# Attention and gated MLP on one core: the second head's softmax scaling in blocks 3 to 5 moved from ScalarE to GpSimd

## The chip, the cores and the metric

The kernel runs on one core of one Trainium2 chip. The metric is device time in microseconds (us) of one execution. The engines are named as in the profile: PE is TensorE's matmul stream and PEld its weight loads, DVE is VectorE, ACT is ScalarE, POOL is GpSimd, SP is SyncE, which here issues the DMAs. SBUF is the on-chip memory; a PSUM bank is where PE writes its results.

## The reference

Attention with a local window and a few global columns, over 4 batches, 8 heads, 768 positions and 64 channels, then a two-layer MLP whose gate is h times sigmoid(h), on 3072 tokens.

```python
scores = scale * np.matmul(q, k.transpose(0, 1, 3, 2))
...
keep = is_global | is_local            # 8 global columns, 96 local positions
...
scores = np.where(keep, scores + bias, -1000000000.0)
a = np.exp(scores - np.max(scores, axis=-1, keepdims=True))
a = a / (np.sum(a, axis=-1, keepdims=True) + 1e-09)
x = np.matmul(a, v)                    # then (B, H, S, D) -> (3072, 512)
...
h = x @ w_in                           # 512 -> 2048
g = h * (1.0 / (1.0 + np.exp(-h)))
return (g @ w_out).astype(np.float32)  # 2048 -> 512
```

The line that the change touches is the division of `a` by its row sums.

## The kernel before

**Tiles.** The queries are cut into 24 blocks of 128 positions (`i`, six to a batch), and the 8 heads of a block into 4 pairs (`hp`), so there are 96 pair steps, numbered `u = 4 * i + hp`. Blocks 3 to 5 are the steps 12 to 23. A block sees 232 columns (96 before it, 8 global, its own 128), so a head's probabilities are a tile of 128 x 232 in float32; the two heads of a pair lie side by side in one tile `pe`.

**A pair step.** PE makes the scores in a bank (L626 in the blocks up to 5). DVE adds the bias and takes the row's extreme (L639, one instruction for each head). ACT takes the exponential and its row sum (L647). DVE adds 1e-9 to the two sums (`guard`, L654) and inverts them (`inverse`, L658). Then `norm` multiplies each head's tile by its inverse sum, one value for each of the 128 rows: head 0 on DVE (L669), head 1 on DVE too, but in blocks 3 to 5 on ACT (L667), which `on_act` and the parameter `NA=(12, 24)` say. PE turns both heads (`turn_p`, L683, up to four transposes into one bank), ACT moves the result to SBUF (`move_p`, L693), and PE multiplies by the values (L708).

**The MLP.** Two blocks make a group of 256 tokens (`g`, 12 groups). The weights come as raw 64-bit words in 32 pieces and are built up by DVE: three bit operations (L416, L422, L428), a rounding copy by ACT (L440) and a subtraction by DVE (L444), which leave a high and a low part of each piece in SBUF. Groups 0 and 1 use the weights as they come: for each of 16 slices `f`, PE makes h with 12 matmuls (L869), ACT and DVE gate it (L875, L879) and split it into two parts (L883, L887), and PE multiplies by the second weight (L894, 6 matmuls). The later groups use another form of the second product (L972, L978, L984, L990, L1020, L1049), in which POOL adds 128 x 128 tiles (L990).

**The order.** Nothing is ordered by hand on an engine. `Plan` is a list scheduler that runs while the program is built: each step has an engine, a planned cost in ns, a rank, the steps that it needs and the buffers that it uses. `run` goes through planned time, gives each free engine the ready step of lowest rank, and emits the steps in that order; on the chip each engine then works through its own queue in that order. A planned cost therefore changes the order on all engines from the first place where it matters. The step of `norm` is made in the loop over `i` and `hp`; `guard` and `inverse` are ahead of it, and `turn_p` needs both heads:

```python
o = op("DVE", 72, u - PAR["RI"], (lambda i=i, hp=hp: inverse(i, hp)), [o], [pe])
...
o = op("PE", 438 if j else 220, u - PAR["RP"], (lambda i=i, hp=hp, tp=tp: turn_p(i, hp, tp)), [*o, joint], [pe, tp])
```

The functions that the diff touches, with what calls them:

Of the kernel before, what the change touches and what calls it, by code (L numbers as in the profile page):

```python
# [17 lines left out]
ALU = mybir.AluOpType  # L18
# [11 lines left out]
PAR = dict(  # L30

    LAT=140, SD=125, DL=1900, D0=2700, DW=2900, DO=3400, MG=60, T2=45000, LAT2=230, MG2=400, F0=600, F1=1200, C1=900, C2=2300, COLD=8000, WEND=8600,

    CAP=dict(po=4, av=2, s=4, h=3, tp=2, tq=4), HU=13,

    C0=14, CR=1, LW=1, LB=5, QB=3.5, RI=2.8, RN=2.8, RP=0.2, RM=0, RV=1.2, RQ=0.1, RB=3, LK=-25, LAG=1,

    BP=(4, 3), NX=20, CF=8, AHEAD=5, SB=(4,), LQ=(1, 2), CN=3, I0=6, QS='ACT', G0=2, TR=10, RL=4500, TL=6000, CL=3200, VC=8, WT=2, HE=1.8, TP=3, ORD=(5, 7, 0, 1, 2, 3, 4, 6), NA=(12, 24), V2=6,
)


# [9 lines left out]
class Plan:  # L51
# [31 lines left out]
    def op(self, eng, cost, rank, emit, deps=(), uses=(), lat=None):  # L83
        o = dict(eng=eng, cost=int(cost), rank=rank, emit=emit, uses=list(uses), lat=lat,
                 need=0, ready=0, then=[], n=len(self.ops))
        o["uses"] += [b.also for b in o["uses"] if b.also]
        for d in deps:
            if d is not None:
                d["then"].append(o)
                o["need"] += 1  # L90
        for b in o["uses"]:
            b.n = min(b.n, len(self.ops))
            b.left += 1
        self.ops.append(o)
        return o
# [90 lines left out]
def attn_moe(ctx, tc, q, k, v, n_global, n_local, w_in, w_out, out):  # L186
    nc = tc.nc
# [3 lines left out]
    NHP = H // 2  # L191
# [165 lines left out]
    op = plan.op  # L357
    FIRST = -1e6
    DVE = lambda n: 1000 * (62 + n) / 960
    ACT = lambda n, over=61: 1000 * (over + n) / 1200  # L360
# [86 lines left out]
    for n in range(2 * NFC):  # L447
        rank = PAR["C0"] + PAR["CR"] * n
        a, m, x = [] if lent(n) is not None else [Buf("big")], Buf("mid", "m"), lent(n)
        o = op("DMA", 1456, rank - PAR["LW"], (lambda n=n: stage(n, "w")), [o_l[x]] if not a else (), a, PAR["DW"])  # L450
        o_st.append(o)
        o = op("DVE", 335, rank, (lambda n=n: conv1(n)), [o], [*a, m])
        o = op("DVE", 602, rank, (lambda n=n: conv2(n)), [o], [*a, m])
        o = op("DVE", 602, rank, (lambda n=n: conv3(n)), [o], [*a, m])
# [32 lines left out]
    for n in range(2 * NFC):  # L487
        a = Buf("ck", "big")
        o = op("DMA", 1456, 1e6 + n, (lambda n=n: stage(n, "c")), [o_c[-4]] if n > 1 else (), [a], PAR["CL"])
# [3 lines left out]
    for n in range(PAR["VC"] // 2):  # L493
        a = Buf("ck", "big")
        o = op("DMA", 1456, 1e6 + 99 + n, (lambda n=n: check_v(n)), [o_c[-1]], [a], PAR["CL"])
# [160 lines left out]
    def inverse(i, hp):  # L656
        t = blk[i]
        nc.vector.reciprocal(t["inv", hp], t["inv", hp])  # L658

    def on_act(u):  # L660
        return (1,) if PAR["NA"][0] <= u < PAR["NA"][1] else ()

    def norm(i, hp, a):
        t = blk[i]
        x = t["p", hp][:, a, :cols(i)[1]]
        if a in on_act(NHP * i + hp):
            nc.scalar.mul(x, x, t["inv", hp][:, a:a + 1])  # L667
        else:
            nc.vector.tensor_scalar(x, x, t["inv", hp][:, a:a + 1], None, ALU.mult)  # L669
# [71 lines left out]
    for i in range(B * NJ):  # L741
        j, g = i % NJ, i // NB
        rank = NHP * i - PAR["QB"]
        ob, kk, lr = o_k[i], kb[i], PAR["LB"]
        if not i:
            xn, later = dict(k=Buf("qkn", "m"), q=Buf("qkn", "m")), []
            for p0, p1 in PARTS:
                for nm in "kq":
                    n, tp = p1 - p0, Buf("tq")
                    hi = kk[nm.upper() + "H"]  # L750
                    o = op("DMA", 364 * n, -8.5, (lambda nm=nm, a=2 * p0, b=2 * p1: load(0, nm, a, b)), (), [xn[nm]], PAR["D0"])
                    rank = 0.2 if p0 else rank
                    o = op("PE", 110 * n, rank, (lambda nm=nm, tp=tp, a=p0, b=p1: turn(0, nm, tp, a, b)), [o], [xn[nm], tp, hi])
# [3 lines left out]
        for nm in "kq" if i else "":  # L757
            xn, tp = Buf("big") if in_kind(i, nm) == "big" else Buf("qkn", "m"), Buf("tq")
            hi, lo = kk[nm.upper() + "H"], kk[nm.upper() + "L"]
            o = op("DMA", 1456, rank - lr if i < NJ + NB else FIRST + rank, (lambda i=i, nm=nm: load(i, nm)), () if i < NJ + NB else [before["t"]], [xn], PAR["DL"])  # L760
# [5 lines left out]
            o = op("PE", 440, rank, (lambda i=i, nm=nm, tp=tp: turn(i, nm, tp)), [o, *own, *o_w[-PAR["WT"]][i != PAR["I0"]:]] if stacked else [o], [xn, tp, hi, lo] if stacked else [xn, tp, hi])  # L766
# [35 lines left out]
        for hp in range(NHP):  # L802
            u = NHP * i + hp
            stacked = i >= PAR["I0"]
            kind = pt_kind(i, hp)
            pe, pt, tp = Buf("pe", "m"), Buf(kind, "m" if kind == "pt" else None), Buf("tp")
            n = cols(i)[1]
            hps = (hp,) if stacked or (not i and hp < 2) else (hp - hp % 2, hp - hp % 2 + 1)
            if hp == hps[0]:
                s = [Buf("s") for _ in range(1 if stacked else 2)]  # L810
                ks = [kk[x] for x in (("KH", "KL", "QH", "QL", "R") if stacked else ("KH", "QH"))]
                before["s"] = o_s[u] = op(
                    "PE", 440 if stacked else 390 + len(hps) * (385 if j else 218), u,
                    (lambda i=i, hps=hps, s=s: stack_scores(i, hps[0], s) if i >= PAR["I0"] else scores(i, hps, s)),
                    [x for y, x in ob.items() if i or y[1] <= hps[-1] < y[2]] + [before.get("s")], s + ks,
                )
            o = before["s"]
            if not u:
                for x in later:
                    plan.after(x, o)  # L820
            if u == PAR["HU"] - 1:
                o["hold"] = 1
            o_e = []
            for a in range(2):
                x = op("DVE", 318 if j else 210, u, (lambda i=i, hp=hp, a=a: top_of(i, hp, a)),
                       [o, o_b[j == 0, hp], before.get("top") if not a else None], [s[a % len(s)], pe])
                if not a:
                    before["top"] = x
                o_e.append(op("ACT", ACT(n, 112) + 186, u, (lambda i=i, hp=hp, a=a: expo(i, hp, a)), [x], [pe]))
            if i >= PAR["VC"] and hp == 1:  # L830
                o_c.append(op("DVE", 598, u + 0.5, (lambda i=i: check_here(i)), [arrived, before["top"]], [kk["vn"]]))
            o = op("DVE", 67, u - PAR["RI"], (lambda i=i, hp=hp: guard(i, hp)), o_e, [pe])
            o = op("DVE", 72, u - PAR["RI"], (lambda i=i, hp=hp: inverse(i, hp)), [o], [pe])
            o = [op(*(("ACT", ACT(n)) if a in on_act(u) else ("DVE", 250 if j else 196)), u - PAR["RN"], (lambda i=i, hp=hp, a=a: norm(i, hp, a)), [o], [pe])
                 for a in range(2)]
            o = op("PE", 438 if j else 220, u - PAR["RP"], (lambda i=i, hp=hp, tp=tp: turn_p(i, hp, tp)), [*o, joint], [pe, tp])
            o_m.append(op("ACT", ACT(512 if j else 256), u - PAR["RM"], (lambda i=i, hp=hp, pt=pt: move_p(i, hp, pt)), [o, before.get("move")], [tp, pt]))
            before["move"] = o_m[-1]
            pts.append(pt)
# [11 lines left out]
        if early:  # L851
            x = Buf("pt", "m")
# [68 lines left out]
    G0 = PAR["G0"]  # L921
# [170 lines left out]
    for m0, n in enumerate(PAR["ORD"]):  # L1092
# [3 lines left out]
        o, run = o_first[-1], []  # L1096
        for m, c in enumerate((690, 423, 423)):
# [4 lines left out]
            o = op("DVE", c, rank, emit, [o, o_w[-1][1]], [rb, tb])  # L1102
        o_p.append(o)
        o = op("ACT", 940, rank, (lambda n=n: t_high(n)), [o], [rb, tb])
        hs = op("DMA", 1456, rank, (lambda n=n: t_store(n, 0)), [o], [rb, tb], PAR["TL"])
        o = op("DVE", 1130, rank, (lambda n=n: t_low(n)), [o], [rb, tb])
# [6 lines left out]
    for g in range(NGRP):  # L1113
# [4 lines left out]
        o = o_h[g - 1, NFC - 1] if g > 1 else None  # L1118
        for f in range(NFC) if g < G0 else ():
            rank = 1e3 + (max(g, 1) * NFC + f + (PAR["LAG"] + 0.5 if g else 0))  # L1120
            ph, th, gh, gl = Buf("h"), Buf("th"), Buf("gh"), Buf("gl")
            for c in range(NCC):
                o = op("PE", 349, rank + PAR["LK"] / 10, (lambda g=g, f=f, c=c, h=ph: moe_h(g, f, c, h)),
                       [o, *o_w[2 * f]] + o_x[g], [ph, xb[g]["xh"], xb[g]["xl"]])
# [3 lines left out]
            t = op("ACT", 340, FIRST + rank, (lambda g=g, f=f, b=th: moe_tanh(g, f, b.slot)), [o], [ph, th])  # L1128
            t = op("DVE", 335, FIRST + rank, (lambda g=g, f=f: moe_gate(g, f)), [t], [ph, th])
# [9 lines left out]
        for n in range(NFC // 2) if g >= G0 else ():  # L1139
# [4 lines left out]
            for c in range(2 * NCC):  # L1144
                o = op("PE", 349, rank + PAR["LK"] / 10 - (PAR["HE"] if end else 0), (lambda g=g, n=n, c=c, h=ph: pair_h(g, n, c, h)),
                       [o] + o_x[g], [ph, sg, xb[g]["xh"], xb[g]["xl"]])
# [7 lines left out]
            t = op("ACT", 600, FIRST + rank, (lambda g=g, n=n: pair_tanh(g, n)), [o], [ph, sg])  # L1154
            t = op("DVE", 690, FIRST + rank, (lambda g=g, n=n: pair_gate(g, n)), [t], [ph, sg])
# [6 lines left out]
            for m, (a, b) in enumerate(cuts):  # L1162
                if b == 7:
                    for e in range(4):
                        x = "DVE" if soon and e != 1 else "POOL"
# [76 lines left out]
        if g < G0:  # L1242
            ob = Buf("big")
            for tt in range(NB):
                eng = "ACT" if tt % 2 else "DVE"
                o = op(eng, dict(ACT=478, DVE=598)[eng], FIRST + rank,
                       (lambda g=g, tt=tt: moe_end(g, tt)), [last[tt]], [po[tt], ob])
# [79 lines left out]
    o = steps(judge, [70, 270, 100, 70, 270, 100, 70, 270, 100, 70, 70, 70, 70, 70, 70, 70], -1, o_c + o_x[-1], ())  # L1327
    o = op("PE", 60, -1, verdict, [o], [jb])
# [190 lines left out]
```

## Time and profile before

| | |
|---|---|
| time, median of 3 runs | 672.51 us (671.33 to 672.54) |
| the profiled execution | 671.82 us, of which the span from its first to its last instruction is 670.0 us |
| PE busy | 660.1 us, 99% of the span |
| DVE busy | 545.1 us, 81% |
| ACT busy | 431.8 us, 64% |
| POOL busy | 154.1 us, 23% |
| granted TensorE clock | 1.00 of full speed over the span |

A matmul's record reaches past the start of the next one, since they are pipelined; so the busy share of PE says that it had something in flight, and its real pace is read from the starts. Records of DVE and ACT overlap a little in the same way: what an instruction takes in a queue is the step from its start to the start of the next.

### The profile page before, as it was taken

What the parts mean: (1) busy time and instruction counts of PE and PEld (TensorE: products, weight loads), DVE (VectorE), ACT (ScalarE), POOL (GpSimd) and SP (SyncE); (2) the same over time, 40 slices, a digit from 0 to 9 for tenths busy, and PEclk for the clock granted to TensorE, in tenths of its full rate; (3) what the DMA queues carried; (4) which work ended last, traced back from release to release, by engine and by line L of the source; (5) the groups of instructions that cost most, each with busy time, mean ns of one, the idle gap of its engine ahead of it and who ended that gap; (6) DMA issues with size and microseconds to landing.
All of it is one profiled execution on the core that took longest, in us unless ns stands there. A gap on an engine that the chain in (4) does not pass through costs nothing.

```text
span 670.0 us, 15715 instructions
## 1 busy us (share of the span) xinstructions
PE 660.1 (99%) x5756; PEld 633.7 (95%) x5756; DVE 545.1 (81%) x1507; ACT 431.8 (64%) x1026; POOL 154.1 (23%) x339
## 2 busy tenths in 40 slices
PE   7999999999999999999999999999999999999997
PEld 5778899999999999999999999999999999999997
DVE  6999999998668888878889878877878887975545
ACT  6997544687567676665775766684667666673333
POOL 2100000010003322324322323323332332322331
PEclk9999999999999999999999999999999999999999
DMA  9997757575887589669687686675876788754442
GB/s 184 235 284 256 230 165 241 167 239 181 239 246 250 168 256 283 196 180 295 186 223 235 202 235 198 211 229 170 288 217 185 226 230 217 226 162 144 126 167 82
DMA packets 146068, 141.63 MB, mean 211 GB/s; under 512 B 88356, under 2 KB 115492, under 8 KB 145988
## 3 DMA queue, kind: packets, MB, share of 16 engines
q1 hardware_dynamic: 145984, 140.60, 70.4%
q8 instruction: 46, 0.75, 0.5%
q14 instruction: 34, 0.28, 0.1%
q10 hardware_dynamic: 4, 0.00, 0.0%
HBM read 117.44 MB, written 18.87 MB: 203 GB/s over the span
## 4 chain that ended last, share of the span: by engine, by line
PE 94%; DVE 4%; ACT 1%; DMA 0%; issue 0%; DVEq 0%; ACTq 0%
PE bank L972 33%; PE bank L1049 29%; PE bank L894 7%; PE bank L869 7%; PE bank L708 5%; PE bank L683 5%; PE bank L596 5%; PE bank L528 2%; DVE pe L639 1%; DVE pe L669 1%; DMA qn<-in_q_dram 0%; ACT pe L647 0%; PE bank L1332 0%; DVE wf L428 0%; DVE wf L422 0%; PE bank L626 0%
## 5 line engine op out<-in xcount | busy, mean ns | idle before, releaser
L990 POOL TENSOR_TENSOR sg<-sg 128x128 f32<-128x128 f32 x279 | 128.9, 483 | 285.4 <-DVE sg L984 232.7
L972 PE MATMUL bank<-xh,WIH 128*128 128x256 f32 x640 | 183.1, 286 | 0.0
L972 PE MATMUL bank<-xl,WIH 128*128 128x256 f32 x640 | 177.8, 278 | 0.0
L972 PE MATMUL bank<-xh,WIL 128*128 128x256 f32 x640 | 177.6, 278 | 0.0
L1020 DVE TENSOR_TENSOR gl<-sg,gh 128x512 fp32r<-128x512 f32 (+1 forms) x152 | 97.6, 647 | 34.4 <-ACT gh L1014 30.6
L972 PEld LDWEIGHTS bank<-xl,WIH 128*128 128x128 f32 x640 | 120.6, 188 | 0.5
L972 PEld LDWEIGHTS bank<-xh,WIH 128*128 128x128 f32 x640 | 120.6, 188 | 0.4
L972 PEld LDWEIGHTS bank<-xh,WIL 128*128 128x128 f32 x640 | 120.3, 188 | 0.0
L1014 ACT CAST gh<-sg 128x512 fp32r<-128x512 f32 (+1 forms) x152 | 83.9, 568 | 52.3 <-PE bank L1049 38.6
L647 ACT ACTIVATE pe<-pe,NM 128x232 f32<-128x232 f32 (+1 forms) x192 | 90.2, 473 | 36.6 <-DVE NM L639 35.8
L978 ACT ACTIVATE sg<-bank 128x512 f32<-128x512 f32 x80 | 47.8, 597 | 48.1 <-PE bank L972 47.5
L639 DVE CUSTOM_DVE_ANT_0 pe<-bank,B 128x232 f32<-128x232 f32 (+1 forms) x192 | 66.5, 373 | 12.6 <-PE bank L596 11.8
L1049 PE MATMUL bank<-WOH,gh 128*128 128x256 f32 (+1 forms) x280 | 74.0, 294 | 0.0
L984 DVE SCALAR_TENSOR_TENSOR sg<-sg,bank 128x512 f32<-128x512 f32 x80 | 54.8, 685 | 23.4 <-ACT sg L978 22.7
L1049 PE MATMUL bank<-WOL,gh 128*128 128x256 f32 (+1 forms) x280 | 72.5, 289 | 0.0
L669 DVE TENSOR_SCALAR pe<-pe,sm 128x232 f32<-128x232 f32 (+1 forms) x180 | 60.5, 370 | 1.4
L683 PE MATMUL bank<-ident,pe 128*128 128x128 f32 (+1 forms) x352 | 55.0, 276 | 3.7 <-DVE pe L669 3.5
L693 ACT COPY pt<-bank 128x512 f32<-128x512 f32 (+1 forms) x82 | 44.7, 549 | 15.1 <-PE bank L683 13.0
L1049 PEld LDWEIGHTS bank<-WOH,gh 128*128 128x128 f32 x280 | 52.8, 188 | 1.5 <-issue 0.7
L1049 PEld LDWEIGHTS bank<-WOL,gh 128*128 128x128 f32 x280 | 52.7, 188 | 0.8
L1049 PE MATMUL bank<-WOH,gl 128*128 128x256 f32 (+1 forms) x280 | 49.5, 292 | 0.0
L683 PEld LDWEIGHTS bank<-ident,pe 128*128 128x128 f32 (+1 forms) x352 | 39.9, 136 | 8.9 <-DVE pe L669 6.1
(165 smaller groups left out, 1509.8 us busy)
## 6 DMA issues: line engine op xcount, KB each, us to landing
tx<-ts SPq DMA_DIRECT2D x72, 512.0 KB
ty<-ts SPq DMA_DIRECT2D x72, 256.0 KB
c<-in_moe_w_in_dram SPq DMA_DIRECT2D x16, 512.0 KB
c<-in_moe_w_out_dram SPq DMA_DIRECT2D x16, 512.0 KB
vn<-in_v_dram SPq DMA_DIRECT2D x24, 256.0 KB
w<-in_moe_w_in_dram SPq DMA_DIRECT2D x12, 512.0 KB
w<-in_moe_w_out_dram SPq DMA_DIRECT2D x12, 512.0 KB
kn<-in_k_dram SPq DMA_DIRECT2D x23, 256.0 KB
```

The lines of the kernel that those rows point to most:

```text
L639: nc.vector.tensor_tensor_reduce(t["p", hp][:, a, :n], t["s", hp][a][:, :n], B1[:, hp] if i % NJ else B0[:, hp], -SC / (1 + a), 3.0e38, AL ...
L647: nc.scalar.activation(x, x, AF.Exp, bias=NM[:, i * H + h:i * H + h + 1], scale=-1.0, accum_out=t["sum", hp][:, a:a + 1],)
L669: nc.vector.tensor_scalar(x, x, t["inv", hp][:, a:a + 1], None, ALU.mult)
L683: nc.tensor.transpose(ps[:n, c, a], pe[:, a, c0:c0 + n], ident)
L869: nc.tensor.matmul(ph, w[:, c, fs], x[:, c], start=not c and not n, stop=c == NCC - 1 and n == 2)
L972: nc.tensor.matmul(ph[:, a], w[:, cc, fs], x[:, cc], start=not cc and not m, stop=cc == NCC - 1 and m == 2)
L978: nc.scalar.activation(x[:, 0:4].rearrange("p (a b) c -> p a (b c)", a=2), mo["ph", g, n], AF.Tanh, scale=0.5)
L984: nc.vector.scalar_tensor_tensor(x, x, 1.0, mo["ph", g, n], ALU.add, ALU.mult)
L990: (eng.tensor_sub if e else eng.tensor_add)(x[:, o], x[:, a], x[:, b])
L1014: nc.scalar.copy(mo["gh", g, n][:, a:b], mo["sg", g, n][:, a + o:b + o])
L1020: nc.vector.tensor_sub(mo["gl", g, n][:, a:b], mo["sg", g, n][:, a + o:b + o], mo["gh", g, n][:, a:b].bitcast(F32))
L1049: nc.tensor.matmul(o, l, r, start=(g, b) not in opened, stop=n == NFC // 2 - 1 and m == 2 and (p in ((2, 7, 5, 3, 4) if g == NGRP - 1 else ...
```

## The change

Head 1 of each pair in blocks 3 to 5 is scaled by a GpSimd `tensor_tensor` product instead of a ScalarE `mul`. Its second input is the column of 128 inverse sums, spread along the row by a step of zero. The planned cost of that step becomes 800 ns on POOL, where it was `ACT(n)`, that is 1000 * (61 + 232) / 1200 = 244 ns, on ACT. `NA` stays as it is, but `on_pool` is asked first, and its range is the same.

```diff
-    ... TP=3, ORD=(5, 7, 0, 1, 2, 3, 4, 6), NA=(12, 24), V2=6,
+    ... NP=(12, 24), HE=1.8, TP=3, ORD=(5, 7, 0, 1, 2, 3, 4, 6), NA=(12, 24), V2=6,
...
+    def on_pool(u, a):
+        return a == 1 and PAR["NP"][0] <= u < PAR["NP"][1]
+
...
-        if a in on_act(NHP * i + hp):
+        if on_pool(NHP * i + hp, a):
+            nc.gpsimd.tensor_tensor(x, x, t["inv", hp][:, a:a + 1].to_broadcast(list(x.shape)), ALU.mult)
+        elif a in on_act(NHP * i + hp):
             nc.scalar.mul(x, x, t["inv", hp][:, a:a + 1])
...
-            o = [op(*(("ACT", ACT(n)) if a in on_act(u) else ("DVE", 250 if j else 196)), ...
+            o = [op(*(("POOL", 800 if j else 500) if on_pool(u, a) else ("ACT", ACT(n)) if a in on_act(u) else ("DVE", 250 if j else 196)), ...
```

## Rows read from the trace of the kernel before

**Rows 1.** Windows: busy us of each engine in three stretches, granted clock, DMA.
```profile
core 0: us, PE busy (x) PEld busy (x) DVE busy (x) ACT busy (x) POOL busy (x), PEclk, DMA share, GB/s
31.00:43.00 12.00, 9.61 (x89) 7.64 (x87) 12.00 (x46) 11.58 (x35) 0.00 (x0) 1.00 0.97 267
43.00:70.00 27.00, 26.80 (x209) 23.70 (x210) 27.00 (x90) 22.10 (x63) 0.00 (x0) 1.00 0.89 268
70.00:118.00 48.00, 48.00 (x314) 43.52 (x313) 48.00 (x104) 23.42 (x53) 0.00 (x0) 1.00 0.66 210
```

**Rows 2.** Waits, 31 to 50 us: who waited for whom, total us, times, longest.
```profile
PE bank L683 <- DVE pe L669: 2.6, 4, 0.8
```

**Rows 3.** Timeline of PE, 80 to 87 us: one slice of the weights.
```profile
80.51 0.39 PE L894 MATMUL bank<-WOH,ghs 128*128 128x512 f32 x1
...
83.78 0.40 PE L894 MATMUL bank<-WOH,gls 128*128 128x512 f32 x1
...
84.95 0.28 PE L869 MATMUL bank<-xh,WIL 128*128 128x256 f32 x1
...
86.12 0.39 PE L894 MATMUL bank<-WOH,ghs 128*128 128x512 f32 x1
```

**Rows 4.** Timeline of DVE, 79 to 85 us: the same slice.
```profile
79.17 0.42 DVE L887 TENSOR_TENSOR gls<-ths,ghs 128x256 fp32r<-128x256 f32 x1
...
82.58 0.42 DVE L887 TENSOR_TENSOR gls<-ths,ghs 128x256 fp32r<-128x256 f32 x1
82.92 0.69 DVE L444 TENSOR_TENSOR WIL<-wf,WIH 128x512 fp32r<-128x512 f32 x1
...
84.79 0.42 DVE L887 TENSOR_TENSOR gls<-ths,ghs 128x256 fp32r<-128x256 f32 x1
```

**Rows 5.** Groups of ACT, 31 to 70 us, and the timeline around the first.
```profile
L667 ACT ACTIVATE pe<-pe,sm 128x232 f32<-128x232 f32 x12 | 5.9, 493 | 0.2 <-DVE sm L658 0.2
...
31.18 0.54 ACT L667 ACTIVATE pe<-pe,sm 128x232 f32<-128x232 f32 x1
31.57 0.66 ACT L440 CAST WIH<-wf 128x512 fp32r<-128x512 f32 x1
```

**Rows 6.** Groups of POOL by form: instructions, busy us, mean ns of one.
```profile
L990 POOL TENSOR_TENSOR sg<-sg 128x128 f32<-128x128 f32 x279 | 128.9, 483 | 285.4 <-DVE sg L984 232.7 <-DVE sm L654 24.2 <-DVE sm L658 16.0
...
L1086 POOL TENSOR_TENSOR ost<-ost 128x256 f32<-128x256 f32 x1 | 0.7, 737 | 3.9 <-ACT ost L1078 3.9
```

**Rows 7.** Timeline of DVE: what follows the reciprocal of two pairs.
```profile
30.93 0.15 DVE L658 RECIPROCAL sm<-sm 128x2 f32<-128x2 f32 x1
31.01 0.37 DVE L639 CUSTOM_DVE_ANT_0 pe<-bank,B 128x232 f32<-128x232 f32 x1
...
31.31 0.33 DVE L669 TENSOR_SCALAR pe<-pe,sm 128x232 f32<-128x232 f32 x1
...
66.39 0.68 DVE L444 TENSOR_TENSOR WOL<-wf,WOH 128x512 fp32r<-128x512 f32 x1
```

**Rows 8.** Timelines of POOL and DVE, 29 to 31 us and 134 to 137 us.
```profile
29.96 0.50 POOL L613 COPY KHw<-KHw 128x384 f32<-128x384 f32 x1
...
29.98 1.02 DVE L428 SCALAR_TENSOR_TENSOR wf<-w,wf 128x512 uint32<-128x512 uint32 x1
...
34.74 0.67 DVE L428 SCALAR_TENSOR_TENSOR wf<-w,wf 128x512 uint32<-128x512 uint32 x1
...
135.20 1.26 DVE L946 TENSOR_TENSOR tsum<-tsum,raww 128x1024 fp32r<-128x1024 f32 x1
135.33 1.50 POOL L613 CAST KL<-KL 128x384 fp32r<-128x384 f32 x1
```

**Rows 9.** Timelines of POOL and DVE, 220 to 223 us.
```profile
220.48 1.87 POOL L990 TENSOR_TENSOR sg<-sg 128x128 f32<-128x128 f32 x4 [4.70 <-DVE sm L654]
...
220.91 1.05 DVE L669 TENSOR_SCALAR pe<-pe,sm 128x232 f32<-128x232 f32 x2
...
222.27 0.59 DVE L669 TENSOR_SCALAR pe<-pe,sm 128x232 f32<-128x232 f32 x2
```

More of the change, by code (lines that the diff above doesn't have):

```diff
@@ L36 @@
     C0=14, CR=1, LW=1, LB=5, QB=3.5, RI=2.8, RN=2.8, RP=0.2, RM=0, RV=1.2, RQ=0.1, RB=3, LK=-25, LAG=1,
-    BP=(4, 3), NX=20, CF=8, AHEAD=5, SB=(4,), LQ=(1, 2), CN=3, I0=6, QS='ACT', G0=2, TR=10, RL=4500, TL=6000, CL=3200, VC=8, WT=2, HE=1.8, TP=3, ORD=(5, 7, 0, 1, 2, 3, 4, 6), NA=(12, 24), V2=6,
+    BP=(4, 3), NX=20, CF=8, AHEAD=5, SB=(4,), LQ=(1, 2), CN=3, I0=6, QS='ACT', G0=2, TR=10, RL=4500, TL=6000, CL=3200, VC=8, WT=2, NP=(12, 24), HE=1.8, TP=3, ORD=(5, 7, 0, 1, 2, 3, 4, 6), NA=(12, 24), V2=6,
 )
@@ L833, in attn_moe @@
             o = op("DVE", 72, u - PAR["RI"], (lambda i=i, hp=hp: inverse(i, hp)), [o], [pe])
-            o = [op(*(("ACT", ACT(n)) if a in on_act(u) else ("DVE", 250 if j else 196)), u - PAR["RN"], (lambda i=i, hp=hp, a=a: norm(i, hp, a)), [o], [pe])
+            o = [op(*(("POOL", 800 if j else 500) if on_pool(u, a) else ("ACT", ACT(n)) if a in on_act(u) else ("DVE", 250 if j else 196)), u - PAR["RN"], (lambda i=i, hp=hp, a=a: norm(i, hp, a)), [o], [pe])
                  for a in range(2)]
```

## The prediction

> **What bounds the kernel now.** I read the windows first, since the shares of the page are means over stages. Blocks 3 to 5 run between 31 and 70 us. In that stretch DVE has no idle time at all, nor has it any up to 118 us [rows 1]: attention and the building of the weights share it. PE has something in flight nearly always from 43 us on, but from 31 to 43 us it is idle for 2.4 of 12 us [rows 1], and the waits say for what: four transposes L683 waited 2.6 us in all, each for the scaled head of DVE, L669 [rows 2]. ACT is almost full too from 31 to 43 us (11.58 of 12) and has room later (22.10 of 27) [rows 1]. POOL does nothing from 31 to 118 us [rows 1].
>
> Then the timelines, to see which of the two full engines sets the pace between 71 and 130 us, while groups 0 and 1 use the weights as they are built. For one slice of the weights PE needs two groups' worth of L869 and L894: from 80.51 to 86.12 us, 5.61 us [rows 3]. DVE needs two pieces and two gates: from 79.17 to 84.79 us, 5.62 us [rows 4]. They run at the same pace, side by side, and what matters is how far DVE is ahead. The gate's low part L887 starts at 82.58 and ends at 83.00 us [rows 4]; the first matmul that reads it starts at 83.78 us [rows 3], a lead of 0.8 us. The low part of a weight piece, L444, ends at 83.61 [rows 4] and its first matmul starts at 84.95 [rows 3], 1.3 us. So DVE is the engine whose lateness counts: it never catches up before the weights are done, and beyond some 0.8 us a delay of DVE in blocks 3 to 5 becomes a delay of PE. PE then has no idle time in which to win it back [rows 1].
>
> **The change, part by part.** *What ACT loses.* Twelve instructions L667 of 493 ns [rows 5]; in the queue one takes the step from 31.18 to 31.57, 0.39 us [rows 5]. So ACT is relieved of 12 x 0.39 = 4.7 us over 39 us. What it feeds in this stretch is DVE (the row sums for L654, the rounding copies for L444), and DVE waits for nothing there. I cost this gain at nothing; the cover is the backlog of DVE. If DVE did have room, the gain would be bounded by PE's idle 2.4 us.
>
> *What POOL gains.* Twelve products of 128 x 232. The trace has the same operation at 128 x 128, 483 ns, and at 128 x 256, 737 ns [rows 6]; on the line between them 232 columns take 483 + 104 x 254 / 128 = 689 ns. No row has an input spread by a step of zero; I take it as an ordinary one, with 483 ns and the planned 800 ns as bounds. As an occupation of POOL that is 8.3 us of 39, and POOL is idle: nothing queues behind the product there.
>
> *What DVE loses.* This is the term that decides. The plan leaves DVE's costs as they are, but the trace shows the two engines holding each other up. A copy of POOL of 0.50 us ran beside an L428 that took 1.02 us, where another took 0.67 [rows 8]: 0.34 us more, 68% of the copy. In the other direction a copy of POOL took 1.50 us beside L946, against 0.50 [rows 8]. Two L669 took 1.05 us beside a train of four additions of POOL, and 0.59 us once the train was over [rows 9]: 0.46 us more, 44% of the 1.05 us that POOL worked beside them. On the other hand L639, which reads a bank, is not stretched.
>
> The new product comes at the worst place. It is released by the reciprocal L658, and right behind L658 stands one instruction and then the L669 of the same pair, in 11 of the 12 pairs. In six pairs the one between is an instruction that reads a bank, 0.30 us long from start to start, as at 31.01 us [rows 7]; POOL starts beside it and is still at work when L669 is due. In the other six it is one that POOL has to wait for, as L444 at 66.39 us [rows 7], and POOL starts when it ends, just when L669 is due again. Priced by the two ratios, 44 to 68% of 0.69 us, one product costs DVE 0.30 to 0.47 us; I take 0.40, in the middle, since both a two-input instruction and L669 will be hit. Twelve make 4.8 us. Below it is bounded by 0.15 us each (1.8 us): the two L669 share 0.46 us, so one is stretched by 0.23, and a product that falls beside an instruction that reads a bank costs less. Above it is bounded by the whole length, 0.69 us each, 8.3 us.
>
> The Trainium skill, SBUF — State Buffer, in "SBUF: two separate sides", says that GpSimd and a VectorE instruction with two SBUF inputs, or in a mode that uses both ports, share one port pair as an exclusive lock, held by whichever starts first for its whole instruction. The trace agrees in kind: 1.50 us against 0.50. In degree it shows less than the whole length, 0.34 us of 0.50. By the rule the loss would be the upper bound, and that is a rival below.
>
> *What else is later.* The transposes of a pair wait for both heads. POOL's head is ready some 0.1 + 0.69 us behind the reciprocal at best, and L669 behind it; now L669 ends at 31.64 us, 0.56 us behind a reciprocal that ended at 31.08 [rows 7]. The plan puts 800 ns on the product, so it will send other work to PE first; before 43 us there is little of it, and there the waits of 2.6 us grow. These are the same delays as DVE's, seen from PE, not further ones. The changed costs also give the list scheduler another order on every engine from step 12 on; DVE's work stays the same, so I put no price on it but some 1 us either way.
>
> **The sum.** 671.8 us (the profiled execution) + 4.8 us of DVE - 0.8 us of lead = 675.8 us. The median of the runs is 0.7 us above the profiled one, so for the median 672.5 + 4.0 = 676.5 us. With the bounds of the port, 1.8 and 8.3 us, it goes from 673.5 to 680.0, and with 1 us for the order from 672.5 to 681.
>
> **The rivals.**
> 1. *The lock holds for the whole instruction.* 12 x 0.69 - 0.8 = 7.5 us: 680.0 us. For it speaks the copy of 1.50 us; against it the two ratios.
> 2. *POOL starves.* DVE sends one two-input instruction after another and POOL gets the port late each time, as with the copy that took 1.0 us more. Then it is the transposes that wait, for POOL. Only those pairs hurt whose transposes PE has nothing to put ahead of; with 1.0 us for each of ten pairs, less the lead, some 9 us: 681.5 us. It decides if products take over 1.2 us. Against it: the L428 that was stretched shows that POOL gets in between two instructions.
> 3. *Hidden.* Products fall beside the instructions that read a bank and cost under 0.15 us each; the lead of 0.8 us swallows half: 672.5 to 673.5 us, no change. Against it: L669 is due 0.3 us after the product starts.
> 4. *Faster, on the other side.* ACT was the true limit from 31 to 43 us: five of the twelve L667 lie there, 2.0 us of ACT, and PE's idle 2.4 us are the room. If exponentials and moves come earlier by that much and DVE is free to take them up, PE gains up to 2 us: 670.5 us. It decides if DVE loses less than ACT's gain brings it. Against it: DVE is not idle for an instant there [rows 1].
>
> **Chances.** Forecast (port, 673.5 to 680) 0.55, rival 1 0.12, rival 2 0.08, rival 3 0.13, rival 4 0.12. About 0.2%, 1.35 us, is what can be told from no change here. Faster by more than that: rival 4, 0.12. Within it: rival 3 and a little of the forecast's low end, 0.15. Slower: 0.73. The range leaves out rival 4 below and the far part of rivals 1 and 2 above: 671.5 to 681.0 us.
>
> **What the profile after would show.** Twelve TENSOR_TENSOR of 128 x 232 on POOL between 31 and 75 us, around 0.7 us if the port is free and over 1 us where they wait; no L667. L669 in blocks 3 to 5 well above 0.33 us [rows 7], or the two-input lines L422, L428, L444 above 0.69 us beside a product, in sum near 5 us. DVE without idle time until past 118 us, and the end of the weights some 4 to 5 us later. PE with new waits for DVE or POOL between 31 and 75 us of about 4 us, and the first L972 later by the same. ACT idle for some 4.7 us more, which brings nothing. Wrong would be the step "DVE's lateness becomes PE's" if DVE shows the loss and the first L972 doesn't move; the price if the lines stay at 0.34 and 0.69 us; and the cost of nothing for ACT if the first L972 comes earlier.

## The result and the profile after

The kernel with the change takes 676.12 us (median of 4 runs, 675.82 to 676.46), the kernel before 672.02 us on the same chip (4 runs): ratio 1.0062, 95% interval 1.0048 to 1.0075. It is 4.1 us slower, where the forecast was 4.0. The profiled execution's span grew from 670.0 to 674.5 us. Line numbers shift with the diff: L667 becomes L670 (now on POOL), L669 becomes L674, L683 becomes L688, L869 becomes L874, L879 becomes L884, L883 becomes L888, L887 becomes L892, L894 becomes L899, L972 becomes L977; L416 to L658 stay.

The same three windows as in [rows 1], of the kernel after (us, then busy time and instructions of PE, PEld, DVE, ACT and POOL, granted clock, DMA share, GB/s):

```profile
31.00:43.00 12.00, 9.26 (x68) 6.79 (x64) 12.00 (x41) 9.83 (x28) 3.89 (x6) 1.00 0.96 280
43.00:70.00 27.00, 25.58 (x222) 22.00 (x222) 26.97 (x86) 19.22 (x55) 4.62 (x7) 1.00 0.79 241
70.00:118.00 48.00, 47.87 (x308) 42.12 (x307) 48.00 (x105) 21.52 (x51) 0.89 (x1) 1.00 0.68 212
```

DVE is as full as before, and gets less done: 41 instructions against 46 in the first 12 us. ACT has lost 1.75, 2.88 and 1.90 us of work in the three stretches, 17 instructions, of which twelve are the scalings; the other five come later. PE is busy for 0.35, 1.22 and 0.13 us less. The granted clock is 1.00 throughout, so it plays no part.

One pair on DVE, and then a second one, in the timeline after (start, us, engine, line, operation, tiles):

```profile
31.05 0.16 DVE L658 RECIPROCAL sm<-sm 128x2 f32<-128x2 f32 x1
31.12 0.38 DVE L639 CUSTOM_DVE_ANT_0 pe<-bank,B 128x232 f32<-128x232 f32 x1
...
31.42 0.64 DVE L674 TENSOR_SCALAR pe<-pe,sm 128x232 f32<-128x232 f32 x1
31.98 0.39 DVE L639 CUSTOM_DVE_ANT_0 pe<-bank,B 128x232 f32<-128x232 f32 x1
```

And POOL's timeline (in brackets its idle time before, and what ended it):

```profile
31.35 0.57 POOL L670 TENSOR_TENSOR pe<-pe,sm 128x232 f32<-128x232 f32 x1 [8.55 <-ACT pe L647]
33.03 0.85 POOL L670 TENSOR_TENSOR pe<-pe,sm 128x232 f32<-128x232 f32 x1 [1.11 <-DVE sm L658]
...
39.97 0.89 POOL L670 TENSOR_TENSOR pe<-pe,sm 128x232 f32<-128x232 f32 x1 [3.08 <-DVE sm L658]
```

It goes as in [rows 7]: the reciprocal, an instruction that reads a bank, the scaling. But the scaling now falls into the product of POOL (31.35 to 31.92), and DVE needs 0.56 us from its start to the next start where it needed 0.25. The scaling alone takes 0.33 us; ending at 32.06 it was let in at 31.73, 0.19 us ahead of the product's recorded end. Over all twelve pairs, in the rows of the two lines (shortest, median and longest ns, and from when to when):

```profile
L674 DVE TENSOR_SCALAR pe<-pe,sm x12: 331/646/702, 31.4 to 72.0; 128x232 f32<-128x232 f32 x12
L670 POOL TENSOR_TENSOR pe<-pe,sm x12: 572/714/891, 31.3 to 71.7; 128x232 f32<-128x232 f32 x12
```

and of the kernel before:

```profile
L669 DVE TENSOR_SCALAR pe<-pe,sm x12: 322/336/346, 31.3 to 69.6; 128x232 f32<-128x232 f32 x12
```

Ten of twelve scalings are stretched; in the other two (at 47.09 and 60.28 us, 0.37 and 0.33 us long) the scaling came only 0.24 and 0.19 us ahead of the product's recorded end. Six products take 0.57 to 0.58 us, six 0.85 to 0.89: these begin beside an instruction with two inputs from tiles, such as L444 at 32.78 us, and POOL itself waits for DVE first. By the group's mean a scaling takes 600 ns, 0.264 us more than before, in sum 3.2 us. No other line of DVE is longer here.

What PE waited for, 31 to 50 us, after (us in total, times, longest), the answer to [rows 2]:

```profile
PE bank L688 <- ACT WOH L440: 0.8, 1, 0.8
PE bank L899 <- ACT ghs L888: 0.8, 1, 0.8
PE bank L688 <- DVE pe L674: 0.6, 1, 0.6
PE bank L874 <- DVE WIL L444: 0.4, 1, 0.4
```

POOL's product is not among them, and these waits of PE add up to 2.6 us, no more than before. From 50 to 75 us PE waits 1.4 us more, where it had no wait before. The loss is easier to see in the chain of work that ended last. By engine, over the whole span, its shares before and after are:

```profile
PE 94%; DVE 4%; ACT 1%; DMA 0%; issue 0%; DVEq 0%; ACTq 0%
```

```profile
PE 88%; DVE 9%; ACT 1%; issue 1%; DMA 1%; DVEq 0%; ACTq 0%
```

and the places where it passes from DVE to PE for good (start, us, what), first before, then after:

```profile
42.89 0.26 DVE pe L669
43.15 0.04 issue
43.19 0.65 PE bank L683 x4
```

```profile
75.85 0.34 DVE ths L884
76.19 0.04 issue
76.23 1.65 PE bank L874 x12
```

Before, PE had work enough from 43.2 us on; after, DVE sets the time until 76.2 us. The last weight piece L444 of this stage, in DVE's timelines before and after:

```profile
129.56 0.69 DVE L444 TENSOR_TENSOR w_last<-wf,w_last 128x512 fp32r<-128x512 f32 x1
```

```profile
132.16 0.69 DVE L444 TENSOR_TENSOR w_last<-wf,w_last 128x512 fp32r<-128x512 f32 x1 [0.36 <-ACT w_last L440]
```

It starts 2.6 us later. And the first matmul of group 2, in PE's timelines before and after:

```profile
138.57 0.28 PE L972 MATMUL bank<-xh,WIH 128*128 128x256 f32 x1
```

```profile
143.72 0.28 PE L977 MATMUL bank<-xh,WIH 128*128 128x256 f32 x1
```

It is 5.15 us later. Some 0.45 us of that was there before 20 us, where the chain has a query load 0.43 us later (from 17.95 to 18.38 us), and in the new order eight score matmuls L596, some 0.9 us by their starts, stand ahead of it that come behind it before, so the span's 4.5 us is the better measure.

### The profile page after: what moved, and what is told of

The parts are those of the page before. It is cut to its first block, busy times and chain, and to the rows that moved or that the text cites. A ratio compares the mean times of both kernels' runs of the same rounds, so it can differ in the third digit from the quotient of the medians.

```text
span 674.5 us, 15735 instructions
## 1 busy us (share of the span) xinstructions
PE 663.8 (98%) x5756; PEld 634.2 (94%) x5756; DVE 548.2 (81%) x1507; ACT 426.6 (63%) x1014; POOL 163.3 (24%) x351
## 4 chain that ended last, share of the span: by engine, by line
PE 88%; DVE 9%; ACT 1%; issue 1%; DMA 1%; DVEq 0%; ACTq 0%
PE bank L977 32%; PE bank L1054 29%; PE bank L899 5%; PE bank L713 5%; PE bank L596 5%; PE bank L874 5%; PE bank L688 4%; PE bank L528 3%; DVE pe L674 2%; DVE pe L639 1%; DVE wf L422 1%; DVE wf L428 1%; DVE wf L416 1%; DVE WIL L444 1%; DMA qn<-in_q_dram 0%
## 5 line engine op out<-in xcount | busy, mean ns | idle before, releaser
L977 PE MATMUL bank<-xh,WIH 128*128 128x256 f32 x640 | 183.0, 286 | 0.0
L977 PE MATMUL bank<-xl,WIH 128*128 128x256 f32 x640 | 177.6, 277 | 0.0
L977 PE MATMUL bank<-xh,WIL 128*128 128x256 f32 x640 | 177.5, 277 | 0.0
L977 PEld LDWEIGHTS bank<-xl,WIH 128*128 128x128 f32 x640 | 120.6, 188 | 0.4
L977 PEld LDWEIGHTS bank<-xh,WIH 128*128 128x128 f32 x640 | 120.5, 188 | 0.4
L977 PEld LDWEIGHTS bank<-xh,WIL 128*128 128x128 f32 x640 | 120.3, 188 | 0.0
L639 DVE CUSTOM_DVE_ANT_0 pe<-bank,B 128x232 f32<-128x232 f32 (+1 forms) x192 | 66.6, 372 | 14.7 <-PE bank L596 13.5
L674 DVE TENSOR_SCALAR pe<-pe,sm 128x232 f32<-128x232 f32 (+1 forms) x180 | 63.3, 386 | 1.5
L688 PE MATMUL bank<-ident,pe 128*128 128x128 f32 (+1 forms) x352 | 54.8, 276 | 2.7 <-DVE pe L674 1.6
L688 PEld LDWEIGHTS bank<-ident,pe 128*128 128x128 f32 (+1 forms) x352 | 40.0, 136 | 8.4 <-DVE pe L674 4.6
```

The costliest lines, as they stand in the source:

```text
L639: nc.vector.tensor_tensor_reduce(t["p", hp][:, a, :n], t["s", hp][a][:, :n], B1[:, hp] if i % NJ else B0[:, hp], -SC / (1 + a), 3.0e38, AL ...
L688: nc.tensor.transpose(ps[:n, c, a], pe[:, a, c0:c0 + n], ident)
L977: nc.tensor.matmul(ph[:, a], w[:, cc, fs], x[:, cc], start=not cc and not m, stop=cc == NCC - 1 and m == 2)
```

## The experiments

The theory: POOL's product holds DVE's scaling up through the port they share, and DVE's lateness becomes PE's. The rivals: the new order costs the time (the change alters the costs that the list scheduler plans with); the transposes wait for POOL; ACT's relief is a gain that hides a larger loss. Each run stands against the kernel before on the same chip: differences in us are those of the medians, and ratio and 95% interval stand beside the time. Line numbers shift a little from run to run, so the scaling on DVE has another line in each kernel.

**Order and product apart.** One kernel has the order of after, and the product back on ACT:

```
-            nc.gpsimd.tensor_tensor(x, x, t["inv", hp][:, a:a + 1].to_broadcast(list(x.shape)), ALU.mult)
+            nc.scalar.mul(x, x, t["inv", hp][:, a:a + 1])
```

> The order of the changed kernel on every engine, but the second head is scaled by ScalarE as before, so GpSimd is left out. Theory (the port: a GpSimd product holds up VectorE's L669 beside it, and VectorE's lateness becomes TensorE's): VectorE's scaling of the first head is back at 0.34 us each, and most of the 4.1 us come back, a time of 671.5 to 673. Rival (the order that the planner wrote for the new costs is what costs): it stays at 675.5 to 676.5 us. A split between them gives 673 to 675.5.

Measured: 674.12 us, 1.0032 [1.0020, 1.0045]. The scaling is back at 333 ns, and still 2.0 us are lost: between the two readings. Part of that may be work of ACT that the plan no longer counts. So a second kernel has the same order and leaves the second head unscaled:

```
-            nc.gpsimd.tensor_tensor(x, x, t["inv", hp][:, a:a + 1].to_broadcast(list(x.shape)), ALU.mult)
+            pass
```

> The order of the changed kernel on every engine, with the second head of blocks 3 to 5 left unscaled, so that neither GpSimd nor ScalarE has the product. It prices the order by itself: the run of that order with the product on ScalarE took 674.1 us, but there ScalarE had work that the plan didn't count. Theory A (the order itself costs some 2 us): 673.5 to 674.5. Theory B (that cost came from ScalarE's uncounted work): 671.5 to 672.8, and then all of the change's cost is GpSimd's.

Measured: 673.33 us (10 runs), 1.0022 [1.0013, 1.0032], between the two theories and nearer the first: the order by itself costs 1.25 us (0.9 to 2.2 by the interval). The product then costs the rest, 4.10 - 1.25 = 2.85 us. The last weight piece and the first matmul of group 2 in this run:

```profile
128.81 0.69 DVE L444 TENSOR_TENSOR w_last<-wf,w_last 128x512 fp32r<-128x512 f32 x1 [0.36 <-ACT w_last L440]
```

```profile
140.42 0.28 PE L977 MATMUL bank<-xh,WIH 128*128 128x256 f32 x1
```

The kernel after has the same order and the product besides. There the last piece starts 3.35 us later than here and the first matmul 3.30 us later: in the same order, DVE's lateness becomes PE's almost one for one. The order's own price is another matter: here the last piece starts 0.75 us earlier than before, so DVE isn't late at that point.

The other way round: the order of before (the POOL entry taken out of the plan), and the product on POOL:

```
-            o = [op(*(("POOL", 800 if j else 500) if on_pool(u, a) else ("ACT", ACT(n)) if a in on_act(u) else ...
+            o = [op(*(("ACT", ACT(n)) if a in on_act(u) else ...
```

> The order of the kernel before on every engine, with the second head's product on GpSimd. Theory (the port): VectorE's scaling of the first head at 0.55 to 0.65 us each, some 3 us of VectorE lost, the time 675 to 677 us. Rival (the order): 671.5 to 673 us. If the transposes wait for GpSimd's head because the order doesn't allow for its 0.57 to 0.9 us, it is above 677 us.

Measured: 678.01 us, 1.0101 [1.0084, 1.0118]. Four of its six runs had 4.6 to 5.2 us outside the span where all other runs here have 1.8, so the spans are compared: 673.1 to 674.2, median 673.7 us, 3.3 more than before's 670.4. With the usual 1.8 us that makes 675.5, within the theory's range. The time outside the span is in no trace and its cause is not known, so the 678 us do not speak for transposes that wait. The scaling has a median of 648 ns. One product took 1.225 us.

**The product in the shadow.** The order and the scaling on ACT as before, and beside them twelve products on POOL of the same shape, on a part of WOL that is not yet written, which nobody reads (the cut leaves out a line that fills it once with ones):

```
+    scr = WOL[:, NFC - NLAST - 1, :WIN]
...
+            nc.gpsimd.tensor_tensor(scr, scr.bitcast(F32), t["inv", hp][:, a:a + 1].to_broadcast([P, WIN]), ALU.mult)
             nc.scalar.mul(x, x, t["inv", hp][:, a:a + 1])
```

> The kernel before, with twelve more GpSimd products of 128 x 232, each released by the reciprocal of its pair, on a tile that nobody reads. ScalarE still scales the second head, and nothing waits for GpSimd. Theory (the port alone): VectorE's scaling of the first head is stretched by 0.25 to 0.3 us in most pairs, and the time rises by 2.5 to 4 us, to 674.5 to 676. Rival (what costs is that the transposes wait for a slower engine, or the order): no change, 671.5 to 673 us.

Measured: 675.0 us, 1.0045 [1.0028, 1.0062], span 673.4. The rows of the two lines, and PE's wait from 31 to 50 us:

```profile
L674 DVE TENSOR_SCALAR pe<-pe,sm x12: 578/638/664, 31.2 to 73.1; 128x232 f32<-128x232 f32 x12
L671 POOL TENSOR_TENSOR WOL<-WOL,sm x12: 574/594/1212, 31.1 to 72.7; 128x232 fp32r<-128x232 f32 x12
PE bank L688 <- DVE pe L674: 3.8, 5, 1.4
```

Nobody needs this product, and the kernel is slower by 2.8 us; the scaling of DVE is stretched as after, in all twelve pairs, and PE waits 1.2 us more for it than in [rows 2]. No instruction waits for this product, so what holds the scaling up is not data, but something that the two engines share. That instructions which read a bank are not held (below) points to the way into SBUF, called the port here. With the old order and the real product the profiled span was 673.4 us too (the medians of the spans are 673.7 and 673.2), and the last L444 and the first L977 start within 0.02 us of each other in the two traces: that transposes also wait for POOL adds nothing that can be told.

**The same at half the width.** As above, with 116 columns:

```
+            nc.gpsimd.tensor_tensor(scr[:, :WIN // 2], scr[:, :WIN // 2].bitcast(F32), t["inv", hp][:, a:a + 1].to_broadcast([P, WIN // 2]), ALU.mult)
```

> As the run with twelve GpSimd products that nobody waits for (675.0 us), but of 128 x 116, half as wide. Theory A (VectorE's scaling waits until the product is over, so the price is the product's end less the moment at which the scaling is due): the product ends 0.2 to 0.25 us earlier, the scaling takes 0.38 to 0.45 us instead of 0.63, and the time is 672.7 to 673.7. Theory B (each meeting costs a fixed amount, whatever the width): as with the full width, 674.5 to 675.2.

Measured: 673.38 us (10 runs), 1.0017 [1.0007, 1.0026]. The rows of the two lines, and the first pair in the two timelines:

```profile
L671 POOL TENSOR_TENSOR WOL<-WOL,sm x12: 379/400/1023, 31.0 to 70.7; 128x116 fp32r<-128x116 f32 x12
L674 DVE TENSOR_SCALAR pe<-pe,sm x12: 383/446/456, 31.2 to 71.1; 128x232 f32<-128x232 f32 x12
```

```profile
31.03 0.38 POOL L671 TENSOR_TENSOR WOL<-WOL,sm 128x116 fp32r<-128x116 f32 x1 [8.50 <-DVE sm L658]
```

```profile
31.16 0.38 DVE L674 TENSOR_SCALAR pe<-pe,sm 128x232 f32<-128x232 f32 x1
```

By the medians the product is 0.194 us shorter (594 to 400 ns) and the scaling 0.192 us shorter (638 to 446): the scaling follows the product's end one for one. Here it ends at 31.54, so it was let in at 31.54 - 0.33 = 31.21, 0.20 us ahead of the product's recorded end, as in the kernel after (0.19). DVE is held through the product to a fixed 0.2 us before its recorded end: in four runs (after, the real product in the old order, the shadow, the half width) it comes out at 0.19 to 0.20 us in every one of the 47 pairs where the scaling was held. Whether POOL lets go that early, or the first 0.2 us of a scaling need no port, these rows don't tell.

**What else is held.** The shadow product now reads the scaled first head, and so starts when the first scaling ends:

```
+            nc.vector.tensor_scalar(x, x, t["inv", hp][:, a:a + 1], None, ALU.mult)
+            nc.gpsimd.tensor_tensor(scr, scr.bitcast(F32), x, ALU.mult)
```

> As the run with twelve GpSimd products that nobody waits for (675.0 us), but each product reads the first head's scaled tile, so it is released by the end of VectorE's scaling of the first head and not by the reciprocal: it cannot fall beside that scaling any more. It then falls beside whatever VectorE does next, about half of it instructions with two SBUF inputs. Theory A (the port is held against instructions with two SBUF inputs as well): they are stretched, VectorE still loses 1.5 to 3 us, the time 673.5 to 675. Theory B (it is the scaling in particular that is hit): under 1 us is lost, 671.7 to 673 us.

Measured: 675.93 us, 1.0057 [1.0041, 1.0073]. Groups of DVE from 31 to 75 us (count, busy us, mean ns of one):

```profile
L671 DVE TENSOR_SCALAR pe<-pe,sm 128x232 f32<-128x232 f32 x12 | 4.0, 331 | 0.0
...
L422 DVE SCALAR_TENSOR_TENSOR wf<-w,wf 128x512 uint32<-128x512 uint32 x7 | 6.1, 877 | 0.0
L444 DVE TENSOR_TENSOR WIL<-wf,WIH 128x512 fp32r<-128x512 f32 x5 | 3.9, 775 | 0.0
L416 DVE TENSOR_SCALAR wf<-wl 128x512 uint32<-128x512 uint32 x4 | 2.7, 666 | 0.1
L894 DVE TENSOR_TENSOR gls<-ths,ghs 128x256 fp32r<-128x256 f32 x7 | 3.4, 483 | 0.0
...
L654 DVE TENSOR_SCALAR sm<-sm 128x2 f32<-128x2 f32 x11 | 2.6, 240 | 0.0
```

```profile
L639 DVE CUSTOM_DVE_ANT_0 pe<-bank,B 128x232 f32<-128x232 f32 x20 | 7.4, 385 | 0.0
L886 DVE SCALAR_TENSOR_TENSOR ths<-ths,bank 128x256 f32<-128x256 f32 x9 | 3.7, 406 | 0.0
```

The scaling is free again, and others pay: before, the same means are 685 (L422), 689 (L444), 427 (L416), 421 (the gate's low part, L894 here) and 164 ns (L654). In each mean only some instructions were held: the two held L416 took 0.88 and 0.95 us, the two held L654 0.56 and 0.65. L639 and the part of the gate that reads a bank (L886 here), 390 and 417 ns before, are not stretched, though some run wholly beside a product, as an L639 of 0.39 us at 58.27 beside a product from 58.18 to 58.87 us. The loss is 3.9 us, more than either theory gave. Moving the product does not save the time, since most of what DVE does here is held when it meets a product. This product, with a full tile as its second input, takes 0.68 us alone and 1.00 where it waits.

**DVE's lateness by itself.** Instead of POOL, DVE does twelve more scalings of the unread tile:

```
+        if not a and on_act(NHP * i + hp):
+            nc.vector.tensor_scalar(scr, scr.bitcast(F32), t["inv", hp][:, a:a + 1], None, ALU.mult)
```

> The kernel before, with twelve more VectorE instructions of 128 x 232 on a tile that nobody reads, one ahead of each scaling of the first head in blocks 3 to 5, some 0.25 us each in its queue, 3.0 us in all. GpSimd does nothing more. Theory (any lateness of VectorE in blocks 3 to 5 becomes TensorE's): slower by 2.2 to 3.5 us, 674.5 to 676. Rival (VectorE is ahead by enough to hide 3 us, and the port hurts in another way): under 1.3 us slower, below 673.5.

Measured: 674.74 us, 1.0044 [1.0027, 1.0061], 2.6 us more. One extra scaling in DVE's timeline, and PE's wait from 31 to 50 us:

```profile
31.52 0.33 DVE L671 TENSOR_SCALAR WOL<-WOL,sm 128x232 fp32r<-128x232 f32 x1
31.77 0.33 DVE L675 TENSOR_SCALAR pe<-pe,sm 128x232 f32<-128x232 f32 x1
```

```profile
PE bank L689 <- DVE pe L675: 3.5, 4, 1.0
```

Each takes DVE 0.25 us from start to start, twelve 3.0 us, of which 2.6 come through (1.8 to 4.1 by the interval).

**ACT's relief by itself.** The order of before, and the second head of these pairs left unscaled:

```
-            nc.scalar.mul(x, x, t["inv", hp][:, a:a + 1])
+            pass
```

> The kernel before with the second head of blocks 3 to 5 left unscaled: the twelve L667 are left out and nothing takes their place, so ScalarE has 4.7 us less to do, in the old order. Theory (ScalarE's relief is worth nothing, since VectorE has a backlog all the while): 671.5 to 672.5 us, within 0.2% of before. Rival (ScalarE limits the stretch from 31 to 43 us): faster by 1 to 2 us, 670 to 671.

Measured: 671.6 us (10 runs), 0.9995 [0.9986, 1.0004]. The window from 31 to 43 us, and PE's wait from 31 to 50 us:

```profile
31.00:43.00 12.00, 9.61 (x89) 7.60 (x87) 12.00 (x46) 10.59 (x31) 0.00 (x0) 1.00 0.94 273
```

```profile
PE bank L683 <- DVE pe L669: 2.6, 4, 0.8
```

ACT has 1.0 us less to do than in [rows 1], and PE's busy time, DVE's count and the wait for DVE are the same to the last digit. The relief is worth nothing that can be told, and a gain of 2 us is out.

**DVE instead of POOL.** Both heads on DVE, and planned so:

```
-    ... NA=(12, 24), ...
+    ... NA=(0, 0), ...
```

> Both heads of blocks 3 to 5 scaled by VectorE (the range for ScalarE is empty), as the plan knows. VectorE has twelve more scalings of 0.25 us, 3.0 us; GpSimd and ScalarE have nothing. Theory (a product on GpSimd costs VectorE as much as doing the work itself): as slow as the changed kernel within 1 us, 674.5 to 676.5. Rival (GpSimd at least saves something): 676.5 or more, or the planned order hides it: under 673.5.

Measured: 675.52 us, 1.0048 [1.0032, 1.0063]. Two scalings in DVE's timeline, and what follows:

```profile
31.30 0.58 DVE L669 TENSOR_SCALAR pe<-pe,sm 128x232 f32<-128x232 f32 x2
31.80 0.15 DVE L654 TENSOR_SCALAR sm<-sm 128x2 f32<-128x2 f32 x1
```

The two take 0.50 us of DVE from start to start; in the kernel after, the one took 0.56. The interval overlaps that of the change. This kernel has an order of its own, whose price is not known; the pair with one order is the padded run and the shadow run, 2.6 and 2.8 us. Both ways say the same: handing the product to POOL costs DVE about as much as doing it.

**The plan told of the port.** The kernel after, with the first head's scaling planned at 550 instead of 250 ns in these pairs:

```
-            ... ("DVE", 250 if j else 196) ...
+            ... ("DVE", (550 if on_pool(u, 1) else 250) if j else 196) ...
```

> The changed kernel, with the plan told of what GpSimd takes from VectorE: in blocks 3 to 5 the first head's scaling is planned at 550 ns instead of 250. The instructions are the same. Theory (the loss is VectorE's time and no order gives it back): 675 to 676.5 us. Rival (the loss comes of an order that was written without it): 673.5 to 674.5 us, at most the 1.3 us of the order come back.

Measured: 674.97 us, 1.0045 [1.0029, 1.0060], scaling 325/644/648 ns. That is 2.7 us above before, between the two readings and just below the first. Perhaps 1.4 us (4.10 - 2.74) of the loss come back; the intervals overlap, so this is not shown.

**Less work for DVE.** The instruction that adds 1e-9 to the sums (L654) left out in all 24 blocks, once with the order of before and once out of the plan too:

```
-        nc.vector.tensor_scalar(t["inv", hp], t["sum", hp], 1e-9, None, ALU.add)
-        nc.vector.reciprocal(t["inv", hp], t["inv", hp])
+        nc.vector.reciprocal(t["inv", hp], t["sum", hp])
```

> The kernel before without the addition of 1e-9 to the row sums (L654 is left out in all 24 blocks; the reciprocal reads the sums themselves), in the old order: VectorE has 24 instructions less up to 70 us, 0.07 to 0.2 us each in its queue. It is the opposite of the padded run. Theory (VectorE's lateness sets TensorE's waits up to some 50 us in the kernel before too, so relief pays): faster by 0.8 to 2.5 us, 669.5 to 671.3. Rival (TensorE is the bound, and VectorE's lateness counts in one direction only): 671.5 to 672.5.

> The kernel before without the addition of 1e-9 (L654), this time left out of the plan too, in all 24 blocks, so that the order is written for the shorter chain. With the old order that edit gave 671.2 us against 672.1. Theory (VectorE's relief pays only where the order lets the chain behind it move up): 669.5 to 671 us. Rival (the stretch before 43 us is held by the chain of scores, exponentials and transposes, and no order gains from VectorE): 671 to 672.5 us. A new order can also lose 1 us by itself.

Measured: with the old order 671.18 us (11 runs), 0.9986 [0.9977, 0.9995], a gain at the low edge of what was expected and too small to be told from no change by this kernel's measure. With the new plan 676.5 us, 1.0064 [1.0050, 1.0077]: with less work for DVE the kernel is 4.3 us slower. Neither theory expected that. It shows that a redrawn order alone can cost as much here as the whole change; what in that order costs it was not looked into.

**One measure through the runs.** Two starts and the span, from one trace of each kernel (us):

| kernel | last weight piece L444 | first matmul of group 2 | span |
|---|---|---|---|
| before | 129.56 | 138.57 | 670.0 |
| old order, real product on POOL | 133.08 | 141.83 | 673.4 |
| old order, shadow product | 133.10 | 141.82 | 673.4 |
| old order, shadow of half the width | 130.90 | 139.62 | 671.4 |
| old order, twelve more scalings on DVE | 132.52 | 141.25 | 672.8 |
| new order, no product | 128.81 | 140.42 | 671.6 |
| new order, product on POOL (after) | 132.16 | 143.72 | 674.5 |

Within one order the first matmul is late by as much as the last weight piece, less 0.05 to 0.3 us. Between the orders the two columns part.

## Why the prediction was right

The total was right and so was the mechanism: the product on POOL holds DVE up, and DVE's lateness becomes PE's. But three terms were off and made up for each other, so that the sum came within 0.1 us is luck.

- **The port's price, 0.40 us each, 4.8 in sum: too high.** It is 600 - 336 = 264 ns each, 3.2 us in sum, below even the 0.30 to 0.47 that the two ratios gave. The product with the spread input takes 0.57 us where it doesn't wait, not the 0.69 interpolated from [rows 6], and the scaling comes only after the product has begun and gets in 0.2 us before its recorded end: 0.57 - 0.07 - 0.19 = 0.31 us in the first pair. In two of twelve pairs it came too late to meet more than the end of the product. The prediction had a two-input instruction and the scaling hit; in this order it was the scaling alone, and the late shadow shows that the two-input lines pay when they come due inside a product.
- **The lead of 0.8 us: too large by the traces.** It was read between 80 and 85 us [rows 3, 4] and applied to delays that begin at 31 us. But from 31 to 43 us PE was waiting for DVE already [rows 2], and has no lead there. By the table, 0.05 to 0.3 us of a late weight piece is swallowed on the way to the first matmul of group 2. The times alone (2.6 of 3.0 us in the padded run, 2.85 of 3.2 in the change) are too coarse to tell 0.4 from 0.8 us.
- **The order at no price, 1 us either way: too low.** By itself it costs 1.25 us, at the edge of what was allowed for it (0.9 to 2.2 by the interval). So the sum is 1.25 us of order and 2.85 of product (3.2 less some 0.35 swallowed), 4.1 us, where the forecast had 4.8 - 0.8. "DVE's work stays the same" was true and no ground for a price of nothing: in the new order without the product the last weight piece comes earlier and the kernel is slower all the same.
- **ACT's relief at nothing: right.** 0.9995 with the work left out, and an unchanged wait. Rival 4, the faster one, is out.
- **Rival 1, the whole instruction.** In kind it is true: DVE is held one for one to the product's end less 0.2 us. The Trainium skill, SBUF — State Buffer, "SBUF: two separate sides", has the lock held for the whole instruction by the one who starts first, and the half-width run agrees, up to the 0.2 us. Only the price of 0.69 us each did not follow, since DVE meets no more than what is left of a shorter product when its scaling is due. The ratio of 68% that the prediction set against this rival is no case against it either: the copy ends at 30.46 us and the L428 at 31.00 [rows 8], so an L428 of 0.67 us was let in at 30.33, 0.13 us ahead of the copy's recorded end. What was missing from 0.50 us was that end, and the 0.02 us by which the copy began first, not a share of the whole.
- **Rival 2, POOL starves.** POOL waits too, 0.3 us in six of twelve products, but stays under the 1.2 us from which this was to decide (one product passed it in each of two other runs, 1.212 and 1.225 us), and PE is never shown waiting for it. The shadow product, which no transpose needs, costs as much as the real one.
- **Rival 3, hidden.** Six products do start beside an instruction that reads a bank, yet in four of them the scaling is due well before they end; only two go nearly free. The cover is too short.
- **The signs to look for.** Products, stretched scalings, a full DVE, idle ACT and a later first L977 came as listed. Two did not. The end of the weights came 2.6 us later, not 4 to 5. And there were no "new waits of about 4 us": PE's waits from 31 to 75 us are 4.0 us, where they were 2.6. In the unchanged order of the shadow run those up to 50 us grew by 1.2 us; in the redrawn order they changed hands, and the chain and the windows told more.
- **The range.** Its low end, 671.5 us, is 1 us below the 672.5 that the sum gives, and the working doesn't say why; the result does not hang on it.

What the redrawn order does that costs 1.25 us is not settled: it isn't DVE's lateness at the end of the weights, and where PE loses the time was not found. A scaling that stays clear of the port (reading a bank, as L639 does) was not tried.

## What to carry to other kernels

An idle GpSimd is no free helper when VectorE is the full engine: here each product, 0.57 us long by itself, took 0.26 us from VectorE, about the 0.25 us it would have spent on the work itself, and taking work from ScalarE brought nothing, since what ScalarE feeds there had a backlog anyway. Where an order is drawn from planned costs, every change of a cost draws a new one, worth 1.25 us here and 4.3 us in another run, so time the new order without the new work, and the new work in the old order, before either is believed. A lead between two engines holds only for the stretch in which it was read.

## What the runs showed of the hardware

- A product on POOL of 128 x 232 took 0.57 us with a second input spread from one column, and 0.68 us with a full tile; 116 columns with the spread input took 0.38 us.
- A VectorE scaling that met a product with the spread input got in 0.19 to 0.20 us ahead of the product's recorded end (47 pairs). Beside the product with a full tile the instructions that were held got in 0.13 to 0.14 us ahead: a product from 71.00 to 71.69 us, and an L422 of 0.68 us that began at 71.11 and took 1.12.
- Not only VectorE instructions with two inputs from tiles are held by POOL: the one-input L416 went from 427 to 666 ns in the mean, and the scaling by a column from 336 to 600. Even L654, with two columns, went from 164 to 240 ns. Those that read a bank were not stretched (390 and 385 ns, 417 and 406).
